# Seeds, sums and the order of pairs in a fused attention and spectral-mix kernel

## The chip, the core and the metric

The kernel runs on one core of one Trainium2 chip. The core has TensorE (PE, with its weight loads shown as PEld), VectorE (DVE), ScalarE (ACT), GpSimd (POOL), SyncE (SP), and 16 DMA engines [...]. The metric is device time in microseconds (us); before the change the median of seven runs is 461.56 us (460.44 to 462.81).

## The reference, cut to what matters

Attention with a decay bias gives `x`; then 64 complex modes of `x` along the sequence are mixed by weights `w_r` and `w_i`, and the result is added to `x` and passed through a residual product with `w_ch`.

```python
B, H, S, D = 8, 8, 576, 64                      # d_model 512, n_modes 64
scores = where(causal, -1e9, q @ k.T / sqrt(D) + minimum(bias, 0))
x = softmax(scores) @ v                         # laid out as B x S x 512

X = np.fft.rfft(x, axis=1)
Xr, Xi = np.real(X[:, :n_modes]), np.imag(X[:, :n_modes])
Yr = einsum('bmd,mde->bme', Xr, w_r) - einsum('bmd,mde->bme', Xi, w_i)
Yi = einsum('bmd,mde->bme', Xr, w_i) + einsum('bmd,mde->bme', Xi, w_r)
Y[:, :n_modes] = Yr + 1j * Yi
y = np.fft.irfft(Y, n=S, axis=1)
u = x + y
out = u + maximum(u @ w_ch, 0)
```

## The kernel before, in words

**Attention.** The batch and two heads at a time make 32 iterations (`n`, four groups `g` of two heads times eight batches `b`). The body of an iteration is written out by hand (lines 527 to 551): scores of head 0 (`scores`, L359 to L373, ending in four exponentials on ACT), the value product of the iteration before (`av`, L394 to L404), transposes of the next q (`transposes`, L324 to L327), scores of head 1, transposes of the next k, the forward transform of the iteration before (`fft`, L418 to L425), `av` of head 0, and the modes that are due (`modes`, L441). [...]

**Modes.** The 64 modes are taken in eight chunks of eight per group of 128 input channels. One chunk needs four weight tiles of 512 KB (real and imaginary, even and odd). The first three groups are summed into `y_acc` inside attention; the last group's eight chunks run after attention.

**The weight stream.** The weights are 128 tiles of 512 KB. POOL issues their loads, and those of q, k and v, in one order (`load`, L217); a load waits until its buffer is free, that is, until the modes have read what was there. In the built program POOL uses eight semaphores in turn for them, so at most eight loads are in flight.

**The result.** The output is computed for 18 pairs of two 128-row tiles: 16 whole ones and two made of the 64-row tails of two batches each. For each pair, `u = x + y` and `z = u @ w_ch` are built in PSUM. `z` is the sum of `x @ w_ch`, which needs attention alone and is made early and kept (`z1`), and of the modes' part. For the modes' part, the rows of each chunk (`yb`, and `vb = yb @ w_ch`) are spread to `yv` by SP (`spread`, L465), where 128 rows hold all chunks of one batch; `add_y` (L674) then multiplies by the inverse transform `G_sb`. The last chunk of the first two pairs is taken from the unspread `yb` and `vb` instead, by a matmul with a constant `Gx_sb` that is nonzero on the rows of one batch (`add_last`, L683).

**How a kept product comes back.** Letters in `ways` say it. `s`: kept as fp32, and ACT copies it into the PSUM tile of `z` (L799). `e`: kept as two fp16 parts (value and remainder, L493 on ACT and L494 on VectorE), and four matmuls with the identity put it back (L803). Six pairs (`first_pairs`) have their product made inside attention's last six iterations (L500 to L516), two 512-column halves each, through the PSUM pool `aux`, which has two buffers and serves `fft` and `modes` too; ten (`late`) have theirs made between the last group's chunks (`work`, L590 to L613). Pairs 0 and 1 are not kept.

**The end** (lines 748 to 829). Chunk 6 is computed and spread. Then u of pair 0 and, ahead of the last quarter of chunk 7 (`meanwhile`), z of pairs 0 and 1 take up chunks 0 to 6 from `yv` (112 rows). Chunk 7 follows: its sum, transposes, product with `w_ch`, and `add_last`. Then a loop over pairs 2 to 17: seed of z, modes' part of z, x and modes' part of u, seed of the next pair if it is an `s`, relu on ACT (L712), sum on VectorE (L727) and the output's DMA from SP (L729). z has two PSUM buffers of a pair each.

The softmax here doesn't subtract the row's maximum and nothing guards it: scores larger than these inputs give would overflow.

## Time and profile before

| what | value |
|---|---|
| median of 7 runs | 461.56 us |
| the profiled execution's own time | 460.44 us |
| its span | 458.7 us |
| PE busy | 341.3 us, 74% |
| DVE busy | 236.9 us, 52% |
| ACT busy | 219.2 us, 48% |
| POOL's DMA queue | 81.81 MB |
| SP's DMA queue | 12.17 MB |
| chain that ended last | DMA 54%, PE 29%, DVE 9% |
| granted TensorE clock, mean | 0.895 |

The profiled execution took 1.8 us more than its span, and 1.1 us less than the median. A busy share is a mean over stages: attention lasts until some 342 us, the last group's chunks until 418 us, and the loop over the pairs until the end. The chain of work that ended last is followed back from the last instruction, at each step to what released it.

### The profile page before, as it was taken

To read this page: it belongs to the slowest core of one execution; us is meant where nothing else is said; L and a number is where in the kernel's file an instruction comes from. 1 tells how busy PE (TensorE), PEld (TensorE's weight loads), DVE (VectorE), ACT (ScalarE), POOL (GpSimd) and SP (SyncE) were. 2 spreads that over 40 slices of the span, in tenths; PEclk is the share of its full clock that TensorE was granted. 3 is DMA by queue.
4 is the path that set the end of the run, shared out by engine and by line. 5 is a ranking of instruction groups with operands and counts; after the bars stand their busy time and mean duration, and the time that the engine had idled before them with its cause. 6 is when DMAs were issued, how large, how long until landed. Compare 5 with 4: busy or idle time off the path is not lost.

```text
span 458.7 us, 10246 instructions
## 1 busy us (share of the span) xinstructions
PE 341.3 (74%) x4169; PEld 218.5 (48%) x4201; DVE 236.9 (52%) x527; ACT 219.2 (48%) x382; POOL 182.9 (40%) x269
## 2 busy tenths in 40 slices
PE   1779888966663978836497667879977669877995
PEld 1456656644442656624365444546644336433432
DVE  7775666653332646614355444456656416541675
ACT  1585875554242747723346435536632220310895
POOL 6755555534345455344454444455232232100000
PEclk9997999997777989977779979889999778997999
DMA  9999999999999999999999999999999999993688
GB/s 178 201 203 203 201 201 204 203 204 204 204 204 201 202 203 203 204 205 204 201 197 204 204 204 203 204 203 202 206 206 214 210 210 210 214 216 76 230 291 316
DMA packets 109487, 94.63 MB, mean 206 GB/s; under 512 B 28480, under 2 KB 104640, under 8 KB 109440
## 3 DMA queue, kind: packets, MB, share of 16 engines
q0 software_dynamic: 98960, 81.81, 112.6%
q1 hardware_dynamic: 10480, 12.17, 8.6%
q8 instruction: 33, 0.54, 0.4%
q14 instruction: 14, 0.11, 0.1%
HBM read 164.66 MB, written 9.44 MB: 380 GB/s over the span
## 4 chain that ended last, share of the span: by engine, by line
DMA 54%; PE 29%; DVE 9%; issue 5%; POOL 2%; ACT 1%; SPq 0%; DVEq 0%; POOLq 0%; ACTq 0%
DMA w_sb<-in_moe_w_i_dram 32%; DMA q<-in_q_dram 13%; DMA w_sb<-in_moe_w_r_dram 5%; PE av_ps L394 4%; PE sc_ps L365 4%; PE tr_ps L324 3%; PE sc_ps L359 3%; PE yp L441 3%; DMA k<-in_k_dram 2%; PE z_ps L674 2%; DVE qtB L327 2%; PE ft_ps L418 2%; DVE qtA L327 2%; PE u_ps L693 2%; PE u_ps L674 2%
## 5 line engine op out<-in xcount | busy, mean ns | idle before, releaser
L373 ACT ACTIVATE p_sb<-sc_ps,cumt_sb 128x576 f16<-128x576 f32 (+1 forms) x256 | 141.9, 636 | 46.6 <-PE sc_ps L365 46.1
L217 POOL DMA_DIRECT2D w_sb<-in_moe_w_i_dram x60 | 45.1, 752 | 82.6 <-PE yp L441 42.4
L217 POOL DMA_DIRECT2D w_sb<-in_moe_w_r_dram x60 | 45.4, 757 | 64.1 <-DMA w_sb<-in_moe_w_r_dram 25.7
L217 POOL DMA_DIRECT2D v<-in_v_dram x72 | 50.8, 707 | 33.6 <-DMA v<-in_v_dram 7.2
L324 PE MATMUL tr_ps<-ident,q 64*64 64x64 bf16 x576 | 17.8, 213 | 52.6 <-DMA q<-in_q_dram 52.6
L359 PE MATMUL sc_ps<-negm,ident 128*128 128x256 bf16 x256 | 56.0, 305 | 0.2
L441 PE MATMUL yp<-w_sb,xs 128*32 128x512 bf16 x480 | 36.7, 407 | 18.9 <-DMA w_sb<-in_moe_w_i_dram 14.7
L327 DVE COPY qtA<-tr_ps 64x576 bf16<-64x576 bf16 x32 | 23.8, 743 | 48.2 <-PE tr_ps L324 48.2
L344 ACT ACTIVATE p<-sc_ps,cumt 128x64 f16<-128x64 f32 x32 | 10.1, 314 | 73.8 <-PE sc_ps L340 73.8
L394 PE MATMUL av_ps<-v,p_sb 128*128 128x65 f16 x1024 | 44.8, 198 | 0.0
L394 PEld LDWEIGHTS <-p_sb 128*128 128x128 f16 x1024 | 39.8, 100 | 4.8 <-issue 0.7
L327 DVE COPY ktA<-tr_ps 64x576 bf16<-64x576 bf16 x32 | 24.0, 750 | 33.1 <-PE tr_ps L324 33.1
L324 PEld LDWEIGHTS <-q 64*64 64x64 bf16 x576 | 13.9, 125 | 55.3 <-DMA q<-in_q_dram 54.3
L365 PE MATMUL sc_ps<-qtB,ktB 128*128 128x64 bf16 (+2 forms) x160 | 35.0, 324 | 3.7 <-issue 2.2
L365 PE MATMUL sc_ps<-qtA,ktA 65*128 65x512 bf16 (+2 forms) x192 | 36.6, 300 | 0.3 <-DVE ktA L327 0.3
L441 PEld LDWEIGHTS <-xs 128*32 128x32 bf16 x512 | 22.7, 169 | 29.2 <-issue 25.7
L399 DVE TENSOR_REDUCE den<-av_ps 128x5 f32<-128x10 f32 x64 | 10.8, 169 | 48.4 <-PE av_ps L394 48.3
L404 DVE TENSOR_TENSOR x_all<-av_ps,rcp 128x320 f16<-128x320 f32 x64 | 31.5, 491 | 2.2
L327 ACT COPY ktB<-tr_ps 64x576 bf16<-64x576 bf16 x32 | 20.3, 635 | 21.4 <-DVE ktA L327 20.5
L365 PEld LDWEIGHTS <-ktB 128*128 128x128 bf16 x192 | 22.6, 118 | 15.2 <-issue 6.6
L324 PE MATMUL tr_ps<-ident,k 64*64 64x64 bf16 x576 | 17.3, 209 | 16.0 <-DVE qtB L327 10.1
L418 PE MATMUL ft_ps<-Ff_sb,x_all 128*128 128x192 f16 (+1 forms) x160 | 24.3, 269 | 1.6 <-DVE x_all L404 1.6
(111 smaller groups left out, 527.2 us busy)
## 6 DMA issues: line engine op xcount, KB each, us to landing
w_sb<-in_moe_w_r_dram POOLq DMA_DIRECT2D x60, 512.0 KB, 11.9
w_sb<-in_moe_w_i_dram POOLq DMA_DIRECT2D x60, 512.0 KB, 11.9
q<-in_q_dram POOLq DMA_DIRECT2D x32, 144.0 KB, 9.8
k<-in_k_dram POOLq DMA_DIRECT2D x32, 144.0 KB, 10.2
v<-in_v_dram POOLq DMA_DIRECT2D x72, 64.0 KB, 9.7
out_dram<-r_sb SPq DMA_DIRECT2D x16, 256.0 KB, 2.1
out_dram<-r_w SPq DMA_DIRECT2D x16, 256.0 KB, 2.6
x_all<-in_moe_w_i_dram POOLq DMA_DIRECT2D x3, 512.0 KB, 9.8
```

Source lines behind the costliest of these rows:

```text
L217: nc.gpsimd.dma_start(out=dst, in_=src)
L324: nc.tensor.transpose(ps[rows, r, :], src[rows, r, :], ident16[rows, rows])
L327: copy(out=dst[n % NQ][rows, :].rearrange("d (p r) -> d p r", r=R), in_=ps[rows].rearrange("d r p -> d p r"),)
L359: nc.tensor.matmul(ps[:, bass.ds(w * S, W)], ident16, negm[:, bass.ts(r, W)], start=True, stop=False, skip_group_check=True,)
L365: nc.tensor.matmul(ps[:, c0 : c0 + i1 - i0], keys[:, w, r, :], qt[:, i0:i1], start=False, stop=True, skip_group_check=True,)
L373: nc.scalar.activation(out=pt[:, poff[x] : poff[x] + S - w * W], in_=ps[:, w * S : (w + 1) * S - w * W], func=ACTF.Exp, bias=cumt_sb[:, x, ...
L394: nc.tensor.matmul(ps[:, I, r : r + NCH], lhsT, rhs, start=(i == 0), stop=(i == len(todo) - 1), skip_group_check=True,)
L399: nc.vector.tensor_reduce(out=den, in_=ps[:, :, 0 : VW : NCH], axis=mybir.AxisListType.X, op=ALU.add)
L404: nc.vector.tensor_tensor(out=x_all[:, g, b, :, D * h : D * h + D], in0=ps[:, :, 1 : NCH], in1=rcp.unsqueeze(2).to_broadcast([P, NT, D]), ...
L418: nc.tensor.matmul(ps, x_all[:nT, g, b, T, :], Ff_sb[:nT, T, :], start=(T == 0), stop=(T == NT - 1),)
L441: nc.tensor.matmul(ps[32 * cg : 32 * cg + 32, :], cols[:, c0 : c0 + 32, c * MC + 2 * cg + par], wt[(g, c, ri, par)][:, cg, :], start=(x == ...
L674: nc.tensor.matmul(dst[x][r, :], G_sb[rows, bass.ds(T * P, r.stop - r.start)], yv[rows, bb, which, :], start=start, stop=True, skip_group_ ...
```

## The change

Three things change.

**The first two pairs take two chunks from their sums.** `Gx` holds two chunks, as 16 rows of each, which are loaded into every eighth row of a tile that VectorE has cleared. u and z of pairs 0 and 1 take chunks 0 to 5 from `yv` (96 rows) and chunks 6 and 7 with `add_last`. The x part of pair 1 and chunk 6's product change places, and u of pair 0 now stands inside chunk 7, ahead of its third quarter.

**A third way of keeping, `f`.** Of a product's value and remainder, each half of the rows is placed so that value and remainder of the same 64 rows lie above each other in one 128-row operand. A constant of two 64x64 identities side by side in rows (`fold16h`) adds them up: four matmuls of 64 columns instead of four of 128. Keeping takes two ACT copies and two VectorE subtractions on 64 rows each per product.

**Another order and other letters.** The pairs with a product from attention (batches 1 to 3) alternate with the others. Those six have `f`, pair 15 has `e`, the other nine have `s`; before, seven had `e` and nine `s`, and of the six from attention four had `s` and two `e`.

```diff
-    Gx_np = np.zeros((2 * MC, B, NF * P), dtype=np.float16)
-    Gx_np[:, 0] = G_np[-2 * MC :, : NF * P]
+    NX = 2
+    Gx_np = np.stack([G_np[2 * MC * c :, : NF * P][: 2 * MC] for c in range(NCK - NX, NCK)], axis=1)
...
-    ident16h = gp.tile([P, P], FP16, name="ident16h")
+    ident16h2 = gp.tile([P, P + P // 2], FP16, name="ident16h")
+    ident16h, fold16h = ident16h2[:, :P], ident16h2[:, P:]
...
-            if x == 3 and meanwhile:
-                meanwhile()
+            if meanwhile and x in meanwhile:
+                meanwhile[x]()
...
-    pairs = [((b, T), (b, T + 1)) for b in range(B) for T in range(0, NF, 2)]
-    for i, b in ((4, 0), (10, B // 2)):
-        pairs.insert(i, ((b, NF), (b + 2, NF)))
+    whole = [[((b, T), (b, T + 1)) for T in range(0, NF, 2)] for b in range(B)]
+    tail_pairs = [((b, NF), (b + 2, NF)) for b in (0, B // 2)]
+    turns = [whole[1] + whole[2] + whole[3], whole[4] + whole[5] + whole[6] + whole[7]]
+    turns[1].insert(1, tail_pairs[0])
+    turns[1].insert(5, tail_pairs[1])
+    pairs = list(whole[0])
+    for t in turns[1]:
+        pairs.append(t)
+        if turns[0]:
+            pairs.append(turns[0].pop(0))
...
-    ways = dict(zip(kept, "esesessesesseses"))
-    first_pairs = [i for i in kept[1:] if pairs[i][0][1] < NF and pairs[i][0][0] <= 4][:6]
+    first_pairs = [i for i in kept if pairs[i][0][0] in (1, 2, 3) and pairs[i][0][1] < NF]
+    ways = {i: "f" if i in first_pairs else "s" for i in kept}
+    for i in (15,):
+        ways[i] = "e"
...
+            for y in range(2):
+                own, other = (slice((P // 2) * h, (P // 2) * (h + 1)) for h in (y, 1 - y))
+                nc.scalar.copy(out=z1s[i][own, y, xx], in_=z[own])
+                nc.vector.tensor_tensor(
+                    out=z1s[i][other, y, xx], in0=z[own], in1=z1s[i][own, y, xx], op=ALU.subtract
+                )
...
-    nc.sync.dma_start(out=Gx_sb, in_=d_Gx)
+    nc.vector.memset(Gx_sb.rearrange("p c t -> p (c t)").bitcast(FP32), 0.0)
+    nc.sync.dma_start(out=Gx_sb[0:P:B], in_=d_Gx)
...
-    GK = P - 2 * MC
+    GK = P - 2 * MC * NX
...
-    for i in range(NPRE):
-        x_transposed(i)
+    x_transposed(0)
     x_times_wch(0, False)
-    yb = modes(NG - 1, c)
-    yt = y_transposed(yb, c)
-    y_times_wch(c, yt)
+    yb6 = modes(NG - 1, c)
+    x_transposed(1)
+    yt = y_transposed(yb6)
     x_times_wch(1, False)
-    start_u(0)
-    add_y(us[0], 0, 0, slice(0, GK))
-    def first_sums():
+    vb6 = y_times_wch(c, yt)
+    def first_u():
+        start_u(0)
+        add_y(us[0], 0, 0, slice(0, GK))
+        add_last(us[0], 0, yb6, c=0)
+    def first_z():
         for i in range(NPRE):
             add_y(z_of(i), i, 1, slice(0, GK))
-    yb = modes(NG - 1, NCK - 1, first_sums)
+            add_last(z_of(i), i, vb6, c=0)
+    yb = modes(NG - 1, NCK - 1, {2: first_u, 3: first_z})
...
     add_y(us[1], 1, 0, slice(0, GK))
+    add_last(us[1], 1, yb6, c=0)
     add_last(us[1], 1, yb)
...
+        elif ways.get(i) == "f":
+            for x in range(2):
+                for y in range(2):
+                    nc.tensor.matmul(
+                        zs[i][(P // 2) * y : (P // 2) * (y + 1), x, :], fold16h, z1s[i][:, y, x, :],
+                        start=True, stop=False, skip_group_check=True,
+                        tile_position=(0, (P // 2) * y),
+                    )
```

## The prediction

> **What bounds the kernel now.** I read the page first, then the chain over the last 60 us, the weight tile's own answer, a table by stage, and the order of time over one attention iteration.

> ```profile
> DMA  9999999999999999999999999999999999993688
> ...
> DMA 54%; PE 29%; DVE 9%; issue 5%; POOL 2%; ACT 1%; SPq 0%; DVEq 0%; POOLq 0%; ACTq 0%
> ```

> The DMA engines are full in 36 of 40 slices: the stream of weights, q, k and v sets the time until about 418 us; then 40 us of compute and output follow. The chain around that border:

> ```profile
> 410.45 0.70 DVE v_sb L635
> 411.15 0.02 issue
> 411.17 5.64 DMA yv<-v_sb
> 416.81 0.04 issue
> 416.85 1.83 PE z_ps L674 x4
> 418.68 0.64 PE yp L441 x3
> ...
> 423.62 0.86 PE z_ps L683 x6
> ```

> It seems that the spread of chunk 6 costs 5.64 us. But what waits behind it? The last step of chunk 7's modes needs the last weight tile. The weight tile's answer (395 to 420 us), and below it the stages (busy us of PE, PEld, DVE, ACT and POOL, then the granted clock, DMA share and GB/s):

> ```profile
> L217 POOL DMA_DIRECT2D w_sb<-in_moe_w_i_dram x1: 742/742/742, 396.5 to 396.5; - x1
> ...
> DMA to landing us min/median/max: 21.9/21.9/21.9
> ```
> ```profile
> 413.00:417.00 4.00, 1.81 (x15) 0.88 (x16) 0.00 (x0) 0.00 (x0) 0.00 (x0) 0.99 0.85 157
> 417.00:424.00 7.00, 6.38 (x28) 2.90 (x27) 1.61 (x4) 0.65 (x2) 0.00 (x0) 0.52 0.11 28
> ```

> Issued at 396.48, it lands at 418.4; its matmuls start at 418.61. So the spread hides behind the last weights almost wholly: without it they could start 0.2 us sooner. The second thing to see is the clock column, 0.52 from 417 to 424: after a stretch in which PE worked 1.81 of 4 us, the serial part between the last weights and the first results ran at half clock.

> Third, attention's last six iterations (n = 26 to 31), where six pairs have their product made:

> ```profile
> 326.96 0.59 ACT L491 COPY z<-z_ps 128x512 f32<-128x512 f32 x1 [0.91 <-PE z_ps L513]
> ...
> 327.60 1.12 PE L441 MATMUL yp<-w_sb,xs 128*32 128x512 bf16 x16 [0.45 <-ACT z L491]
> ...
> 328.38 0.75 POOL L217 DMA_DIRECT2D w_sb<-in_moe_w_i_dram  x1 [6.95 <-PE yp L441]
> ```

> PE waits for the copy because the next `yp` takes the PSUM buffer of the product; POOL waits for `yp` because it frees weight buffers. From 306 to 336 PE is busy 8.45, 9.18 and 9.31 of each 10 us: these iterations have no slack on PE.

> [...] states change in steps of 3.41 us, and each window at full clock with PE busy under 0.4 of it was followed by half clock, the one at 0.51 too (413.5 to 416.9), those at 0.53 to 0.59 not; between 0.42 and 0.51 it went both ways. [...] The trace: a group of four 64-column matmuls of 512 takes 0.55 us, against 0.43 for two full ones, plus 0.09 on entry (tail pair, 430.09 to 431.74). [...] here the first packet came 1.45 us after the start of the first issue (1.25 to 2.70).

> **Part 1, constants.** Gx goes from 128 KB to 32 KB, the identity from 32 KB to 48 KB: 80 KB less at some 206 GB/s (the page's mean) is 0.4 us of stream; I take 0.3. The memset on VectorE (a 128x512 fp32 fill; not in the trace; the nearest row is a 128x512 copy at 0.69[...]) stands behind attention's last copies, before the first `y_sb`, and SP's Gx load now waits for it. PE idles 9 of 30 us between 346 and 376, which hides it; without that cover it costs at most 0.7.

> **Part 2, chunk 6 from its sums.** The first sums now wait for chunk 5's spread (landed 408.7), so the 5.64 us disappears from the chain; the last weights take its place: gain 0.2. The two new matmuls per sum (eight of 0.216, 1.7 us) fall, but for two, into the wait before 418. The two are for u of pair 1, later: +0.43. The order now spreads PE's work: chunk 7's first two quarters (0.45 each), six matmuls of u (1.3) from about 413, the third quarter at 415.5 when its weights land, eight matmuls of z (1.7) until 417.5. A 3.41 us window there holds about 2.2 us, or 0.65 busy, against 0.51 before, so I expect full clock. Then the serial part shrinks: quarter 0.64 to 0.45, transposes with u 1.57 to 0.9, v 1.72 to 0.9, first z 0.86 to 0.7: from 5.87 (418.61 to 424.48) to 4.05, gain 1.8. If the clock drops all the same, it is 0.

> **Part 3, the last loop.** Before: seven seeds on PE of 0.866 (four 0.216). After: one such and six fold seeds. A fold seed is four 64-column matmuls, 0.55 + 0.09 = 0.64 (bounds: [...] 1.07 if the halves don't overlap). Pair 2's seed moves to ACT: behind relu of pair 1 (ends 426.08), 1.02 long, so its z starts at 427.1 instead of 426.54: +0.6, with u of pair 1 inside. From there to pair 15 seeds cost 0.87 + 6 x 0.64 = 4.71 against five of 0.866 = 4.33: +0.4. After relu of pair 15 ACT's chain seed 17, relu 16, relu 17 and the last finish sets the end: 450.64 to 455.27, 4.63 before, some 4.4 after, so dropping pair 16's PE seed buys only 0.2. ACT stays under PE: two pairs need three operations of 0.95 to 1.02, at most 3.07, PE 3.2. Output is written at 512 KB per 1.6 us, 330 GB/s; the best two microseconds show 404. Sum: +0.7 (with the two bounds of the fold: -0.6 to +3.3).

> **Part 4, products in attention.** Before, four pairs kept theirs by one ACT copy (0.59), two (n = 28, 31) by ACT and VectorE (0.59 + 0.69). Now each does two copies and two subtractions per product, on 64 partitions each, which I price as on 128. In the built order the second copy waits for the first subtraction, so they run in series: 2 x (0.59 + 0.69) + 0.1 = 2.66 us.
> - First product: `yp` starts 2.0 us later (n = 28, 31: 1.3), and on VectorE the next transposed copy (0.69) is queued behind both subtractions.
> - Second product: ACT's exponentials of the next iteration are queued behind its second copy, 1.3 later; PE needs their score buffers and has 0.4 of slack: +0.9.

> So an iteration grows by 2.9, or by 2.2. n = 26 and 27 vanish in PE's waits for q (3.24 at 287.5 and 2.18 at 299.9) but for 1.0. `yp` is late by 1.0 + 1.3 = 2.3 in n = 28, 5.2 in 29, 8.1 in 30, 10.3 in 31. Besides, PE now idles 2.5 us in one piece in front of each `yp`, enough for half clock for two windows in some three phases of four. At half clock these pieces take 1.08 for 0.66 (av), 0.69 for 0.47 (q transposes), 0.63 for 0.39 (x transposes), about 2 us in 6.8; three iterations times three quarters times 2, rounded down: 4. `yp` of n = 31 is then 14.3 late.

> What is late next is POOL's issue of the four weight tiles at 338.04. By their completion marks the five tiles then in flight end at 351.0, 1.2 of it Gx and the first spread, which would now come later. Cover 11.8, less 1.45 to the first packet: 10.3. The stream stands still for 14.3 - 10.3 = 4.0 us, and nothing gives that back: it has no other gap. PE's lag itself is worked off from 346 to 376 (9 us idle, 3.4 lost to half clock).

> **Sum.** +4.0 (stream) - 0.3 (bytes) - 0.2 (spread) - 1.8 (clock) + 0.7 (loop) = +2.4. The profiled execution took 460.44 with a span of 458.7: 462.8 with 461.1. The median shown lies 1.1 higher, at 461.56, so 464.0.

> **Rivals.**
> - The slip stays inside the queue's cover. It decides at 10.3 us for `yp` of n = 31, just what I get without half clock in attention. Then -0.3 - 0.2 - 1.8 + 0.7 = -1.6: 460.0, faster. For it: the clock term is the least certain. Against: four serial operations are in the order, and PE has no slack there.
> - Stream in time, but half clock after 417 once more: +0.2, 461.7. [...] Against: 0.65 busy.
> - Fold seeds without overlap, the rest as in the first rival: 6 x 0.43 = +2.6, so +1.0: 462.6. The tail pairs' 0.55 speaks against it.

> **How the numbers follow.** Stream late: 0.55, itself 462 to 467.5 (stall 2 to 7.5). The rivals: 0.25, 0.13, 0.07. Faster needs under 460.6 (0.2%, 0.9 us, is about what this kernel's measurement can tell): most of the first rival, 0.22. Within: the second and the edges, 0.22. Slower: 0.56. From 459.8, just under the first rival, to 467.5 lie 8 in 10.

> **What would show it.** Right: the last weight tile lands near 422; DMA falls under 9 tenths near 350; the second ACT copy of a product begins after the first subtraction; `yp` waits over 2 us for VectorE; clock 1.0 in the serial part; no wait for `yv<-v_sb` there; L839 on 64 columns near 0.6 per pair. Wrong: last landing at 418 (the first rival), the clock at 0.5 after it (the second), or fold groups of 1 us (the third).

## The result, and the profile after

The changed kernel takes **464.06 us** (median of 14 runs, 462.31 to 466.61); the kernel before, in runs beside it, 461.33 us (35 runs). The ratio is **1.0062, 95% interval 1.0045 to 1.0080**: slower by some 2.8 us. The prediction was 464.0. The profiled execution of after took 463.34 us with a span of 461.5 us; that of before 460.44 with 458.7.

The page of after, slices of the span and the chain's shares. The two lines to lay beside before's are DMA and the chain:

```profile
DMA  9999999999999999999999999999999999996697
GB/s 173 200 203 203 201 202 203 203 204 204 204 204 200 203 200 204 203 205 204 201 197 205 204 204 204 204 202 203 200 160 170 210 210 214 210 217 126 225 336 271
...
DMA 46%; PE 32%; DVE 10%; ACT 5%; issue 4%; POOL 2%; SPq 0%; DVEq 0%; POOLq 0%; ACTq 0%
```

The digits of DMA hardly tell: a slice is 11.5 us wide. The rates beneath do: 160 and 170 GB/s in the thirtieth and thirty-first slice (335 to 358 us), amid 200 and more. A finer table of DMA, 330 to 358 us in 40 slices of 0.7 us, first before, then after:

```profile
GB/s 209 205 218 200 203 203 209 206 202 208 209 206 205 212 203 205 205 211 206 200 209 217 249 233 193 206 221 247 208 205 209 212 206 208 208 203 205 209 203 203
```
```profile
GB/s 206 208 203 208 205 206 208 205 206 208 171 94 64 42 44 151 176 192 198 181 195 205 203 209 206 211 208 205 206 193 28 7 101 159 181 200 187 196 205 208
```

The stream nearly stands still twice, from 337 and from 351 us. Against 206 GB/s, what the slices lack adds up to 2.6 us of stream in the first hole and 2.0 in the second.

The chain of waits of after around the border between stream and compute:

```profile
401.17 21.71 DMA w_sb<-in_moe_w_i_dram
422.92 0.47 PE yp L444 x4
...
424.95 0.45 PE v_ps L809 x4
...
428.75 0.93 ACT z_ps L828
429.72 0.59 PE z_ps L699 x2
```

The last weight tile lands at 422.88 us (before: 418.4), and nothing stands between it and its matmuls; the spread of chunk 6 is gone from the chain. `v`, two groups of four matmuls that together took 1.72 us before, has one of them here at 0.45. The stages (busy us of PE, PEld, DVE, ACT and POOL, granted clock, DMA share, GB/s) show why:

```profile
413.00:417.00 4.00, 3.55 (x24) 1.59 (x25) 1.74 (x4) 0.59 (x1) 0.00 (x0) 1.00 1.24 206
417.00:423.00 6.00, 4.20 (x30) 1.75 (x25) 0.53 (x1) 0.00 (x0) 0.00 (x0) 1.00 0.88 166
423.00:428.00 5.00, 4.29 (x31) 2.48 (x31) 2.22 (x6) 1.90 (x5) 0.00 (x0) 1.00 0.18 47
```

The clock is 1.00 where it was 0.52. Last, one attention iteration of after in order of time (n = 30, first product):

```profile
335.17 0.58 ACT L515 CAST z<-z_ps 64x512 f16<-64x512 f32 x1 [0.76 <-PE z_ps L537]
335.78 0.68 DVE L516 TENSOR_TENSOR z<-z_ps,z 64x512 f16<-64x512 f32 x1 [0.66 <-ACT z L515]
336.50 0.58 ACT L515 CAST z<-z_ps 64x512 f16<-64x512 f32 x1 [0.75 <-DVE z L516]
337.11 0.69 DVE L516 TENSOR_TENSOR z<-z_ps,z 64x512 f16<-64x512 f32 x1 [0.65 <-ACT z L515]
...
337.86 1.12 PE L444 MATMUL yp<-w_sb,xs 128*32 128x512 bf16 x16 [2.50 <-DVE z L516]
...
338.65 0.75 POOL L220 DMA_DIRECT2D w_sb<-in_moe_w_i_dram  x1 [11.03 <-PE yp L444]
```

Copy, subtraction, copy, subtraction stand in series, each on half the partitions and each as long as on all of them (before: 0.59 for a copy, 0.69 for a subtraction). PE waits 2.50 us for the last, and POOL issues the next weights at 338.65 where before it did at 328.38.

With the ends of the three stages from both traces, the loss is accounted for:

| stage | predicted | before | after | difference |
|---|---|---|---|---|
| until the last weight tile lands | +3.7 | 418.40 | 422.88 | +4.5 |
| from there to pair 2's z | -1.4 | 8.25 | 6.84 | -1.4 |
| from there to the end of VectorE | +0.2 | 28.62 | 28.30 | -0.3 |
| sum (rounded there to +2.4) | +2.5 | 455.27 | 458.02 | +2.75 |

### The profile page after: what moved, and what is told of

Read it like the earlier page. It is cut to its first block, busy times and chain, and to the rows that moved or that the text cites. A ratio compares the mean times of both kernels' runs of the same rounds, so it can differ in the third digit from the quotient of the medians.

```text
span 461.5 us, 10303 instructions
## 1 busy us (share of the span) xinstructions
PE 344.6 (75%) x4177; PEld 218.4 (47%) x4209; DVE 246.8 (53%) x544; ACT 225.9 (49%) x394; POOL 182.9 (40%) x269
## 4 chain that ended last, share of the span: by engine, by line
DMA 46%; PE 32%; DVE 10%; ACT 5%; issue 4%; POOL 2%; SPq 0%; DVEq 0%; POOLq 0%; ACTq 0%
DMA w_sb<-in_moe_w_i_dram 17%; DMA q<-in_q_dram 10%; DMA w_sb<-in_moe_w_r_dram 10%; DMA k<-in_k_dram 7%; PE av_ps L397 4%; PE sc_ps L368 4%; PE yp L444 3%; PE tr_ps L327 3%; PE sc_ps L362 3%; PE z_ps L537 3%; PE ft_ps L421 2%; ACT z L515 2%; DVE z L516 2%; ACT p_sb L376 2%; PE z_ps L625 2%
## 5 line engine op out<-in xcount | busy, mean ns | idle before, releaser
L444 PE MATMUL yp<-w_sb,xs 128*32 128x512 bf16 x480 | 38.3, 440 | 20.5 <-DVE z L516 12.5
L444 PEld LDWEIGHTS <-xs 128*32 128x32 bf16 x512 | 21.5, 173 | 30.4 <-issue 13.7
L515 ACT CAST z<-z_ps 64x512 f16<-64x512 f32 x24 | 13.9, 581 | 36.8 <-PE z_ps L537 27.8
```

The costliest lines, as they stand in the source:

```text
L444: nc.tensor.matmul(ps[32 * cg : 32 * cg + 32, :], cols[:, c0 : c0 + 32, c * MC + 2 * cg + par], wt[(g, c, ri, par)][:, cg, :], start=(x == ...
L515: nc.scalar.copy(out=z1s[i][own, y, xx], in_=z[own])
```

## The experiments

The theory is that two things of opposite sign happen. Keeping halves (`f`) in attention makes the stream stall, which costs over 4 us. Part 2 fills a wait with PE's work and thereby keeps the clock up, which gives back nearly 2. The rivals are that the stall has another cause (cleared tile, order of pairs), that half clock was not the reason for the long serial part, and that folding is dear on PE itself. Ratios are against runs of the kernel before on the same chip, whose median was 460.90, 460.96 or 461.66 us there; small differences between experiments are therefore better read from the ratios than from the times.

### Whole parts in attention (e1)

```diff
-    ways = {i: "f" if i in first_pairs else "s" for i in kept}
+    ways = {i: "e" if i in first_pairs else "s" for i in kept}
```

> The kernel after, with the six pairs of attention kept as one copy and one subtraction on 128 partitions (`e`) in place of two and two on 64 (`f`). Theory (the four serial operations made the stream stall): only four of six products grow, by one subtraction of 0.69 us, so `yp` of n = 31 is some 3 us late, inside the queue's cover. Last weight tile lands near 418.2, no dip of DMA at 338 or 351; six seeds of 0.87 in place of about 0.65 in the last loop, +1.3. Time 461.0. Rival (the stall comes from the cleared tile and its later load, or from the new order of the pairs, both kept here): last landing 422 to 423 and, with the dearer seeds, 465.

Measured: 460.51 us (22 runs), ratio 0.9991 (0.9978 to 1.0003). The same table of DMA from 330 to 358 us:

```profile
GB/s 202 205 205 214 200 208 205 211 202 205 208 208 208 203 202 211 205 209 208 203 206 208 205 208 215 211 215 240 230 211 209 209 206 203 208 209 203 208 206 205
```

Both holes are gone, and the last tile lands at 418.25 us. Cleared tile, later `Gx` load and new order of the pairs are all still in this kernel, so none of them stalled the stream. Some 4.6 us of earlier landing turned into 3.5 us of time, because six whole seeds stand where folded ones stood: from pair 2's z to the end of VectorE 29.97 us against 28.30, so a fold saves 1.67 / 6 = 0.28 us each (up to pair 15's seed, with PE alone in the chain, 23.10 against 21.42 us, the same saving).

### Both copies ahead of both subtractions (e2)

```diff
             for y in range(2):
                 own, other = (slice((P // 2) * h, (P // 2) * (h + 1)) for h in (y, 1 - y))
                 nc.scalar.copy(out=z1s[i][own, y, xx], in_=z[own])
+            for y in range(2):
+                own, other = (slice((P // 2) * h, (P // 2) * (h + 1)) for h in (y, 1 - y))
                 nc.vector.tensor_tensor(
```

> The kernel after, with both copies of a product ahead of both subtractions. The second copy waits for nothing on VectorE any more, but the first subtraction now waits for both copies, so the four operations stay in series and `yp` still waits 2.5 us; only ScalarE is free 0.65 earlier for the exponentials of the next iteration. Theory (an iteration grows by `yp`'s wait and by the late exponentials): `yp` of n = 31 some 2 us earlier than after, stall near 3, last landing near 421.3, time 463.0. Rival (it is `yp`'s wait alone): last landing 422.9, time 464.1.

Measured: 463.08 us (22 runs), ratio 1.0044 (1.0031 to 1.0057). The time is the theory's, but its interval overlaps with after's (1.0045 to 1.0080), and the trace is not what was expected: in the profiled execution, the longest of its runs at 465.02 us, POOL's issue of n = 31 came at 352.55 us, later than after's 350.90, and the last tile landed at 424.57, later than after's 422.88. TensorE had half clock from 296 to 306 us here, full clock in after, and `yp` of n = 28 already starts 2.9 us later than there (312.23 against 309.32). A fairer partner is the trace of e5 below, which has after's order of copies and half clock at the same places: from `yp` of n = 28 to that of n = 31 it takes 40.11 us (311.71 to 351.82), here 39.54 (312.23 to 351.77). So in these two traces the earlier copies gain 0.6 us, where I had expected 2.

### Part 2 alone (e3)

The kernel before with `Gx` for two chunks, the new order of the last chunks and the added `add_last`; pairs, ways and seeds as before.

```diff
-    GK = P - 2 * MC
+    GK = P - 2 * MC * NX
...
-    yb = modes(NG - 1, NCK - 1, first_sums)
+    yb = modes(NG - 1, NCK - 1, {2: first_u, 3: first_z})
```

> The kernel before with the first two pairs' last two chunks from their sums (parts 1 and 2), and nothing else. Theory: landing at 418.1 (bytes -0.3), the next matmuls 0.2 sooner, the serial part at full clock (-1.8), two more matmuls in u of pair 1 (+0.4): 459.4, clock 1.0 after the last landing. Rival (the clock is a matter of chance and halves again): 461.0 to 461.3.

Measured: **458.97 us** (8 runs, 458.59 to 459.13), ratio **0.9946 (0.9927 to 0.9965)**: faster than both kernels. The chain of waits:

```profile
396.07 21.96 DMA w_sb<-in_moe_w_i_dram
418.08 0.48 PE yp L441 x3
...
420.11 0.45 PE v_ps L785 x4
...
421.50 0.81 PE z_ps L684 x6
422.31 0.43 PE u_ps L694 x2
```

From the last weights' matmuls to the end of z of pairs 0 and 1 are 4.23 us; before they were 5.87.

### The two kinds of pairs swapped (e4)

```diff
-    ways = {i: "f" if i in first_pairs else "s" for i in kept}
-    for i in (15,):
-        ways[i] = "e"
+    ways = {i: "s" if i % 2 else "f" for i in kept}
```

> The kernel after with the two kinds of pairs swapped: pairs of attention kept by one fp32 copy (`s`), the late ones as folded halves (`f`). Theory: no slip in attention, last landing near 418; the serial part as in after (4.1 us); eight fold seeds of about 0.65 in the last loop, where before had seven of 0.87 (-0.7 up to pair 15); the late keeps' extra operations (about 2 us of ScalarE and 2.6 us of VectorE for each of eight pairs) fall between 346 and 400, where VectorE and ScalarE are under half busy. Time 458.5. Rival (these operations hold back the chunk steps past 418): 461 or more, with the wait ahead of chunk 7's steps on VectorE or ScalarE in place of a DMA.

Measured: 462.40 us (22 runs), ratio 1.0026 (1.0010 to 1.0043): my forecast of 458.5 fell, the rival holds. The chain of waits:

```profile
404.97 1.01 ACT y_acc L513
406.01 1.23 DVE y_acc L514
407.26 1.02 ACT y_acc L513
408.30 1.24 DVE y_acc L514
...
410.90 3.39 PE z_ps L623 x8
414.29 1.18 PE yp L444 x16
...
423.88 0.43 PE yp L444 x4
```

A late product is twice as wide, so its four serial operations take 4.5 us. They hold its PSUM buffer and stand in ScalarE's and VectorE's queues ahead of the copies that the chunk steps need. And the wait costs PE a second time: busy to 0.14 in the window of 3.41 us from 407.7 us, it then has half clock, and eight matmuls take 3.39 us that took 1.74 at 403.21. The last weights, issued at 400.82, landed 16.9 us later, at 417.7; PE came to them only at 423.88. What I took for cover, the low load of both engines on average, hid nothing.

### The same order with whole parts (e8)

e4 with whole parts for the eight late pairs.

```diff
-    ways = {i: "s" if i % 2 else "f" for i in kept}
+    ways = {i: "s" if i % 2 else "e" for i in kept}
```

> e4 with the eight late pairs as whole parts (`e`) in place of folded halves (`f`): one copy of 1.02 and one subtraction of 1.24 us for each keep where e4 had two of each in series. Theory (the late folds' operations held back the chunk steps and the last weights in e4): landing back near 418.2, no wait ahead of chunk 7 on VectorE or ScalarE; eight seeds of 0.87 in the last loop, one more than before, so 461.2 - 2.0 + 0.7 = 459.9. Rival (it is e4's new order of the pairs): 462.4 plus 1.5 for the dearer seeds, 463.9.

Measured: 460.07 us (22 runs), ratio 0.9971 (0.9961 to 0.9982). The chain has no ScalarE or VectorE ahead of the last weights any more:

```profile
397.68 21.57 DMA w_sb<-in_moe_w_i_dram
419.28 0.47 PE yp L444 x4
```

So it was the late folds that cost e4 its gain, not the order of the pairs, though a whole seed is the dearer one on PE (by 0.28 us in e1). The last tile lands at 419.24, 1 us later than forecast, which stays unexplained.

### Part 2 undone in the kernel after (e5)

```diff
-    GK = P - 2 * MC * NX
+    GK = P - 2 * MC
...
-    add_last(us[1], 1, yb6, c=0)
```

and the order of chunks 6 and 7 as before.

> The kernel after with chunk 6 read from its spread rows again, as before, the order of that stretch with it (part 2 undone; constants, order of the pairs, folded products and the last loop stay). Theory: stall as in after, last landing 422.9; part 2 is worth what it brought alone (e3: 461.3 to 459.0), so 464.1 + 2.0 = 466.1. Rival (what part 2 brings is lost once the stream is late anyway, since chunk 6's spread has longer to land): 464.1 to 464.6.

Measured: 466.62 us (6 runs), ratio 1.0139 (1.0117 to 1.0162), 2.6 us above after. By another way than with a punctual stream, part 2 is thus worth something with a late one, too:

```profile
419.77 5.25 DMA yv<-v_sb
...
425.06 1.02 PE z_ps L699 x4
426.09 0.43 PE yp L444 x4
```

The last tile landed at 424.64 us, so this time the spread sets the end (425.02), and the four sums queued behind it (1.02 us) delay the last quarter as well, at full clock. But not all of the difference belongs to part 2. The profiled executions are 3.1 us apart. From the last landing to pair 2's z it takes 8.21 us here and 6.84 in after: 1.4 for part 2. The other 1.8 us is the landing itself (424.64 against 422.88). It comes out of attention, which is written the same in both kernels: `yp` of n = 28 starts 2.4 us later here (311.71 against 309.32), after half clock from 296 to 306 us where after had full clock. Whether that is chance, though all six runs lie above 466 us, stays open. The theory's number is met, its reason for this kernel isn't.

### PE kept busy ahead of the border (e6 and e11)

In the kernel before, u of pair 0 begins with two matmuls of 0.216 us on x. They are repeated, each time from the start, so that only PE's time changes.

```diff
-        for x, (b, T) in enumerate(pairs[i]):
+        for x, (b, T) in times * list(enumerate(pairs[i])):
...
-    start_u(0)
+    start_u(0, 5)
```

> The kernel before with the x part of u of pair 0 (two matmuls of 0.216 us) computed five times over, each time from the start, ahead of the wait for chunk 6's spread: 1.7 us more of PE work in the window of 3.41 us that was busy to 0.51, in a stretch where PE idles. Nothing else moves. Theory (half clock was what made the serial part 5.87 us long): full clock after 417, serial part near 4.4 (the last quarter's group still stands behind the sums of pair 1), time 459.8. Rival (the shorter serial part of after and e3 comes from the order and the spread rows): no change, 461.0.

> As e6, with the two matmuls done nine times over (3.5 us more), which fills PE from 412.6 to the sums at 416.9 wherever the window falls. Theory (half clock after a window too idle): full clock after 417 in every run, so the runs lie close together (e3's eight within 0.6 us; before's span 4 us), at 459.4. Rival (the added work only shifts chance): spread as before, or slower than e6 because the sums come later.

Measured: with five times (e6) 459.87 us (22 runs), ratio 0.9975 (0.9963 to 0.9988); with nine times (e11) 459.44 us (13 runs, 458.68 to 460.45), ratio **0.9960 (0.9946 to 0.9973)**. Adding work makes the kernel faster. The stages of the first, then of the second:

```profile
413.00:417.00 4.00, 3.36 (x23) 1.40 (x22) 0.00 (x0) 0.00 (x0) 0.00 (x0) 1.00 0.91 176
417.00:423.00 6.00, 4.64 (x23) 2.51 (x23) 1.18 (x3) 0.65 (x2) 0.00 (x0) 0.72 0.16 35
```
```profile
413.00:417.00 4.00, 4.00 (x22) 1.76 (x24) 0.00 (x0) 0.00 (x0) 0.00 (x0) 1.00 0.95 179
417.00:423.00 6.00, 5.12 (x43) 2.83 (x40) 1.60 (x4) 0.96 (x3) 0.00 (x0) 1.00 0.18 40
```

### PE kept busy in attention (e7)

The kernel after with the second transposition of each product in attention five times over.

```diff
-                first_transposed(i, 1)
+                first_transposed(i, 1, 5)
```

> The kernel after with the second transposition of each product in attention (four matmuls of 128x128, 0.4 us) done five times over: 1.6 us of PE work in the gap ahead of `yp` that lets the clock drop; the copy that waits for it stands behind the subtractions anyway. Theory (half clock makes up a part of the slip, my estimate was 4 us of 14.3): full clock from 309 to 354, `yp` of n = 31 some 2 us earlier, stall near 3, last landing 421 and time 462.3. Rival (the slip is the four operations alone): landing 422.9, 464.1, or later by what the added work costs.

Measured: 462.79 us (8 runs), ratio 1.0040 (1.0020 to 1.0059). The stage 306 to 336 us of after, then of this kernel:

```profile
306.00:336.00 30.00, 22.24 (x265) 13.24 (x265) 18.78 (x39) 15.72 (x29) 9.22 (x13) 0.89 1.26 202
```
```profile
306.00:336.00 30.00, 23.06 (x332) 16.17 (x330) 20.53 (x41) 16.28 (x30) 9.70 (x15) 1.00 1.27 204
```

`yp` of n = 28 to 31 begins at 309.19, 322.00, 334.81 and 347.05 us here, in after at 309.32, 323.65, 337.86 and 350.11, in before at 307.74, 317.67, 327.60 and 337.25. The four operations alone make it 9.8 us late in n = 31; half clock in the gaps that they open adds 3.1 in these two executions. The stream at this smaller slip:

```profile
GB/s 205 208 203 206 217 202 202 209 161 105 146 168 183 199 205 202 208 199 211 209 206 221 200 200 208 186 73 72 114 136 195 205 187 200 202 202 211 209 208 200
```

Both holes are shallower (0.9 and 1.6 us against 206 GB/s) and the last tile lands at 420.87. They are not gone, though 9.8 is less than the 10.3 us of cover that I had given the queue.

The end of this execution holds a surprise. Part 2 is in place, and still the serial part behind the last weights runs at half clock:

```profile
420.91 0.47 PE yp L444 x4
...
423.47 1.72 PE v_ps L809 x8
```

PE was busy to 0.42 in the window from 418.5 to 422.0 us, and half clock followed. From the last weights' matmuls to the end of the first z it takes 5.17 us (420.91 to 426.08), in after's trace 3.81 (422.92 to 426.73). So the order of part 2 does not secure the clock when the stream is late, and of the 2.0 us of earlier landing only 0.65 are left at pair 2's z (429.07 against 429.72).

### Folds only where PE waits anyway, and fewer seeds (e9 and e10)

Two versions built on e3, for what might be had beyond it: folded halves for the pairs of n = 26 and 27 alone, and five seeds on PE in place of seven. The first also takes over the code and the constant for folds.

```diff
-    ways = dict(zip(kept, "esesessesesseses"))
+    ways = dict(zip(kept, "efsfssessesseses"))
```
```diff
-    ways = dict(zip(kept, "esesessesesseses"))
+    ways = dict(zip(kept, "esssessessessess"))
```

> e3 with folded halves for the two pairs of n = 26 and 27 alone, where PE waits for q anyway, and seven seeds on PE as before: ways e f s f s s e s s e s s e s e s for pairs 2 to 17. Theory: no stall (landing near 418.2), two seeds at 0.65 in place of 0.87: 458.5, against 459.0 for e3. Rival (folds early in attention still push a later issue past its cover): landing past 419, 460 or more.

> e3 with five seeds on PE in place of seven (pairs 2, 6, 9, 12, 15), the others one ScalarE copy each. Theory (PE sets the last loop, busy 12.0 of each 12 us): -1.7, 457.3. Rival (ScalarE, busy 10.7 of 12 in e3, becomes the bound; two more seeds are 2.0 us of it): 458.5 to 459.5, with PE waiting for ScalarE in the last loop.

Measured: with two folds (e9) 458.76 us (10 runs), ratio 0.9951 (0.9935 to 0.9968); its last tile lands at 418.28, so nothing stalls, and from pair 2's z to the end of VectorE it takes 28.01 us against e3's 28.57: two folds, 0.28 each once more. The gain in time over e3, 0.2 us, lies inside the intervals. With five seeds (e10) 458.99 us (6 runs), ratio 0.9952 (0.9935 to 0.9969), the rival's figure. The stage 424 to 452 us, in e3 and then with five seeds:

```profile
424.00:452.00 28.00, 27.99 (x137) 11.44 (x134) 20.09 (x32) 24.69 (x26) 0.00 (x0) 1.00 0.85 301
```
```profile
424.00:452.00 28.00, 27.00 (x131) 10.97 (x128) 20.39 (x34) 26.84 (x29) 0.00 (x0) 1.00 0.85 300
```

Six matmuls fewer on PE and three operations more on ScalarE in that stage: PE is no longer full, ScalarE is at 26.84 of 28. From pair 2's z to the end of VectorE it takes 27.96 us against e3's 28.57, so of the forecast 1.7 us 0.6 came in the trace, and nothing in the median. That ScalarE would fill up is what the rival said; nothing here separates its own rate from the waits between the two engines.

## Why the prediction was right

The time and the direction were right, and so was the main mechanism: four operations in series delay the release of weight buffers until the stream stalls, and e1, which has one copy and one subtraction in their place, has no stall. Two steps came out right partly by luck: the size of the stall, where two errors nearly cancel, and the full clock behind the last weights. Point by point:

- **Four operations in series** (2.66 us per product): right. The trace has 335.17 to 337.80, 2.63, with halves at 0.58 and 0.68 to 0.69. That an operation on half the partitions costs as much as one on all (before: 0.59 and 0.69) was an assumption; it held.
- **The slip of `yp`** without half clock, 2.3, 5.2, 8.1 and 10.3 us: measured in e7 1.5, 4.3, 7.2 and 9.8. The growth per iteration (2.9, 2.9, 2.6 against 2.9, 2.9, 2.2) was nearly right; from n = 26 and 27 less was left over than the 1.0 us that I had let through.
- **Half clock in attention**, 4 us, an estimate from before's windows: measured 3.1, over two windows at half clock by n = 31 in the profiled execution. e7, in which the clock is 1.00 from 306 to 336 us against 0.89, shows the mechanism. The size belongs to the execution: in the profiled ones of e2 and e5 `yp` of n = 31 comes 1.7 us later than in after's.
- **The cover**, 10.3 us in n = 31, and none needed earlier: wrong twice, in opposite senses. The sixteen completion marks of one tile lie up to 4.5 us apart in before's trace (346.5 to 351.0), and I had counted to the last. From their mean, 348.6, the cover of n = 31 is 348.6 - 338.04 - 1.45 = 9.1. And n = 30, which I took as safe, has 337.6 - 328.38 - 1.45 = 7.8 by the same reckoning: `yp` 10.3 late there makes 2.5, the trace has 2.6. In n = 31 12.9 of slip meet 9.1 and the 2.6 already lost: 1.2, and up to 1.2 more for `Gx` and the spread, which now come later; the trace has 2.0. The sum, 4.6, came near my 4.0 by luck, because one stall too few was set against a cover too long. Even the mean is an estimate that was made after the result and fits only this kernel: e7 is 7.2 us late in n = 30, within 7.8, and still loses 0.9. Counted to the first of the sixteen marks the cover is 335.95 - 328.38 - 1.45 = 6.1 in n = 30 and 346.55 - 338.04 - 1.45 = 7.1 in n = 31; e7 passes both.
- **The rival "slip inside the cover"** (460.0, from 10.3 us down): its threshold falls with that. e7 has a slip of 9.8 and still stalls for 2.5 us. What lies inside the cover is e1's slip of 0.4 us (`yp` of n = 31 at 337.69).
- **Part 1**: the cleared tile took 0.48 us at 359.14 us, under the 0.7 that I had allowed, and stood in nobody's way (e1 keeps it).
- **Part 2, clock**: 5.87 to 4.05 forecast; 4.23 in e3, where it can be read from the chain, and with e11 shown to be the clock. That 0.65 of busy PE is enough rested on before's trace, in which 0.53 to 0.59 kept the clock; in others up to 0.65 lost it. In after the last two windows ahead of the landing were busy to 0.99 and 0.67, in e3 the last one to 0.57, and both kept the clock. The rival "half clock after 417 once more" didn't happen in the profiled execution of after, but it did in e7's, with the same order behind the same late stream: there the window had 0.42. So the full clock in after's was partly luck, and in how many of its other runs it held isn't shown.
- **Part 3, the last loop**: a fold seed at 0.64 against 0.866, a saving of 0.23; measured 0.28. In the chain of after four of the six groups take 0.55 and two 0.43, with 0.54 for the sum behind each. From pair 2's z to the end it is -0.3 in place of +0.2. The rival "folds without overlap" would have shown groups near 1 us: none is there.
- **Of what was to be seen**, all but one came: DMA near 350 us shows no digit under 9 on the page, since the slice is wider than the hole; the rates show it.

## What to carry to other kernels

A wait that opens on TensorE can cost twice: itself, and half clock after it (9.8 and 3.1 us in attention here). Where TensorE must wait ahead of a serial stretch, give it work there, useful or not, and enough of it wherever the window falls: five repeats left a window at 0.53 and lost the clock in the profiled execution, nine kept it. And ask of every operation put ahead of a buffer's release how far ahead the queue behind that buffer is filled; count to the first of the sixteen marks (6.1 and 7.1 us here), not to the last, and check every issue, not only the latest one.

## What was not expected

- Doing two matmuls eight times more than needed made the kernel before 1.8 us faster (ratio 0.9960).
- The sixteen completion marks of one weight tile lie up to 4.5 us apart in before. Behind the first stall of after a tile's marks lie within 0.6 us, 351.1 to 351.7.
- The runs of before lie between 458.5 and 463.0 us, those of e3 between 458.6 and 459.1, those of after between 462.3 and 466.6. In before's profiled execution half clock followed the window from 413.5 us, busy to 0.51; that before's spread comes from where this window falls is a guess, since only one execution of each kernel is profiled.
